# A reordered ramp: powers of lam from the mask's rows, small operations on GpSimd, wide row sums, unread products ahead of a norm

## The chip, the cores and the metric

The kernel runs on one core of a Trainium2 chip. The time is that of one execution in device microseconds, and the number that counts is the median of several runs.

## The reference, cut to what matters

A retention layer (linear attention with a decay lam per head, four sequences of 768 positions, eight heads of 64) is followed by a normalised, gated MLP over all 3072 rows of 512 numbers.

```python
# per head, block b of 64 positions; Dmask[i, j] = lam**(i-j) for i >= j, else 0
intra = ((qb @ kb.T) * Dmask) @ vb
inter = (qb * lam**(pos + 1)) @ kv_state
out[b] = intra + inter
kv_state = lam**64 * kv_state + (kb * lam**(63 - pos)).T @ vb
...
# x: 3072 x 512, the heads' outputs side by side
rms = sqrt(mean(x * x, axis=-1) + 1e-06)
xn = x / rms * rms_g
y = (silu(xn @ w_gate) * (xn @ w_val)) @ w_out          # 512 -> 1536 -> 512
```

## The kernel before, in words

The 3072 rows are six groups m of 512 (four chunks of 128). The 1536 hidden features are twelve blocks f of 128. A unit (m, f) is `Hidden`: `gate` and `val` each multiply a weight block by x in three parts of four passes (part 0: high weight by high x, part 1: low weight by high x, part 2: high weight by low x; f16 halves), `silu` and `mul` join them, `high` and `low` split the product again, and `out` adds it, for each t of four row chunks, to the accumulators acc in PSUM.

The attention of a group is done by `Pair` (m, p), two heads at a time: `scores` (tile pa), `decay_a` (pa times the mask, into a), `decay_k` and `decay_q` (k times lam's power of the last position, q times the powers pw), `state_sums` (pst), `states` (the running state, chunk after chunk), `mix_chunks` (a times v into po), `mix_states` (state times q, added to po), `keep_output` (po into x) and `keep_squares` (po squared, into sq). `scores` of all pairs use one PSUM buffer with the tag ps.

`Norm` makes xn: row sums of the squares (pss), `mean`, `root` (a power on GpSimd, into y), `spread` (y over the partitions by matmuls, pr), and for each block kk of 128 columns `scaled` (xn), `high` (a cast by ScalarE) and `low` (the rest, a subtraction).

`Weights` f turns the raw 64-bit weights into f16 halves: `lift` (ScalarE), `convert` (VectorE, two instructions), `square` and `norm` (a sum of squares, pn), `scale`, `high` (ScalarE), `low` (VectorE), `undo` (two tiny operations that make cg, the factor taken back behind the gate); `lift_o`, `convert_o`, `high_o`, `low_o` do the same for the output weights.

Before the steady loop stands `ramp`: the first two groups' attention, the conversion of the first weights and the units (0, 0) to (0, 5), written out call by call. The order of the calls is the order of each engine's instructions, since the schedule is manual. An engine takes them strictly in that order, and waits at each for its operands. `load_next` issues the next transfer of the list `pending` on SyncE's queue; the tile it loads to is one of four buffers with the tag in, which must be free.

`powers` makes the mask's rows (lam to the power of the distance) and the powers pw by VectorE's scans. `busy(n)` issues n products of the identity with itself into a PSUM tile (unread) that nothing reads.

The ramp ends with the gate of the first unit of group 1; from there on the loop runs the remaining units, and the order there is the same in both kernels.

Of the kernel before, what the change touches and what calls it, by code (L numbers as in the profile page):

```python
# [23 lines left out]
def retention_swiglu_kernel(  # L24
# [117 lines left out]
    def busy(n):  # L142

        ps = ps_out.tile([P, DM], F32, tag="po2", name="unread")
# [10 lines left out]
    def powers(p, part):  # L155
        if part < 2:
            h = 2 * p + part
            nc.vector.tensor_tensor_scan(
                mask[:, h, :], lam_b[:, h : h + 1].broadcast_to([P, P]), ident, 0.0,
                ALU.mult, ALU.add,  # L160
            )
        else:
            nc.vector.tensor_tensor_scan(
                pw[:, p, :], lam_p[:, p : p + 1].broadcast_to([P, P]), zeros, 1.0,
                ALU.mult, ALU.add,
            )
# [23 lines left out]
    def scales_of(pmax):  # L190
        nc.vector.tensor_reduce(gmax, pmax[:, :P], axis=mybir.AxisListType.X, op=ALU.max)
        nc.vector.tensor_single_scalar(ge, gmax.bitcast(I32), 0x7F800000, op=ALU.bitwise_and)
        nc.vector.tensor_scalar_min(ge, ge, float(252 * EXP))
        nc.vector.tensor_scalar(sx.bitcast(I32), ge, -1.0, float(253 * EXP), ALU.mult, ALU.add)
        nc.vector.tensor_scalar(gs, gcol, sx, XS, ALU.mult, ALU.mult)
        nc.vector.tensor_scalar_add(cx.bitcast(I32), ge, float(EXP))
        nc.vector.tensor_scalar_mul(cx, cx, 1.0 / (XS * WS))
# [15 lines left out]

    zeros = wg[:, NF - 1, 1].bitcast(F32)[:, :P]
    nc.scalar.mul(zeros, ones, 0.0)
# [142 lines left out]
    class Weights:  # L358
# [79 lines left out]
        def undo(self):  # L438
            inv = small.tile([P, 2], F32, tag="inv", name=f"inv_{self.f}")
            nc.vector.tensor_scalar_add(inv.bitcast(I32), self.e2, float(64 * EXP))  # L440
            nc.vector.tensor_scalar_mul(cg[:, self.f, :], inv, cx)
# [19 lines left out]
    class Pair:  # L461
# [48 lines left out]
        def states(self):  # L510
            m, p = self.m, self.p
            for c in range(GC):
# [4 lines left out]
                if g % SEQ_CH == 0:  # L517
                    nc.vector.tensor_copy(new, self.pst[:, c, :])
                else:
# [49 lines left out]
        def keep_squares(self):  # L569
# [4 lines left out]
            if m and p == 0:  # L574
# [10 lines left out]

    class Norm:


        def __init__(self, m):
            self.m = m  # L590
            self.x, self.sq = rows.pop(m)
# [6 lines left out]
        def sums(self, i=0):  # L598

            if i == 0:  # L600
                if self.m:
                    pss = ps_att.tile([P, 2, G], F32, tag="ps", name=f"pss_{self.m}")[:, 0]
                else:
                    pss = ps_out.tile([P, DM], F32, tag="po2", name=f"pss_{self.m}")
                self.pss = pss
            sq = self.sq[i]

            n = 1 if self.m else P
            for c in range(GC):
                nc.tensor.matmul(  # L610
                    self.pss[:, c * n : (c + 1) * n], sq[:, c, :], ones[:, :n],
                    start=i == 0 and c == 0, stop=bool(i or self.m), skip_group_check=True,
                )
            self.pss4 = self.pss[:, : GC * n].rearrange("p (c i) -> p c i", c=GC)[:, :, 0]

        def mean(self):
            m = self.m
            self.ms = small.tile([P, GC], F32, tag="ms", name=f"ms_{m}")
            nc.vector.tensor_scalar(self.ms, self.pss4, 1.0 / DM, 1e-6, ALU.mult, ALU.add)
# [197 lines left out]
    def ramp():  # L817
# [7 lines left out]
        powers(0, 0)  # L825
        powers(2, 0)
# [506 lines left out]
```

## Time and profile before

| | us |
|---|---|
| median of 3 runs | 677.46 (677.24 to 678.6) |
| the profiled execution, its time | 678.01 |
| its span, first to last instruction | 676.2 |
| TensorE busy | 666.9 |
| VectorE busy | 324.1 |
| ScalarE busy | 248.4 |
| GpSimd busy | 72.2 |

An execution's time is 1.8 us above its span. A timeline row is a run of like instructions of one engine on one tile: start, duration of the row, engine, line, operation, tiles, shapes, count, and in brackets the idle time ahead of it with what ended it. A matmul's duration holds its way through the array, so rows overlap by up to 0.2 us, and the cost of a row to TensorE is the distance from its start to the next row's start. An f32 matmul appears as two passes.

### The profile page before, as it was taken

Reading aid. Unit: us, or ns where it says so; the run is one execution under the profiler, and the core shown is the slowest. Engines: PE = TensorE matmul, PEld = TensorE weight load, DVE = VectorE, ACT = ScalarE, POOL = GpSimd, SP = SyncE. Lnnn points to the kernel's source line nnn. Section 1 sums busy time; section 2 is a strip of 40 time slices with the busy share of each in tenths; the row PEclk is TensorE's granted clock in tenths of the full one; section 3 lists DMA queues with packets and bytes.
Section 4 is the critical chain, followed back from the end, with each engine's and each line's share of the span. In section 5 each row is a group of like instructions: output and inputs, shape, how many; then the busy total and the mean of one; then the engine's idle time right before and its main releaser. Section 6 shows DMA issues by size and latency. Waiting matters only on the chain.

```text
span 676.2 us, 9894 instructions
## 1 busy us (share of the span) xinstructions
PE 666.9 (99%) x4138; PEld 356.3 (53%) x4138; DVE 324.1 (48%) x579; ACT 248.4 (37%) x439; POOL 72.2 (11%) x71
## 2 busy tenths in 40 slices
PE   7999999999999999999999999999999999999997
PEld 6845665555566444554444555444465444444443
DVE  6797867777546386332812322631331462211112
ACT  3687636776425435322213222221331221211111
POOL 2300000011214303230000111000011000000000
PEclk9999999999999999999999999999999999999999
DMA  8937702541014201122001122100100000100001
GB/s 319 348 128 271 280 25 94 188 156 63 1 63 165 86 0 63 64 94 94 1 0 54 30 105 78 48 0 1 63 1 1 1 0 1 63 0 1 0 1 63
DMA packets 14300, 50.97 MB, mean 75 GB/s; under 512 B 1712, under 2 KB 1968, under 8 KB 12848
## 3 DMA queue, kind: packets, MB, share of 16 engines
q1 hardware_dynamic: 13968, 49.69, 20.4%
q10 hardware_dynamic: 288, 0.66, 0.3%
q8 instruction: 32, 0.52, 0.3%
q14 instruction: 12, 0.10, 0.1%
HBM read 44.05 MB, written 6.29 MB: 74 GB/s over the span
## 4 chain that ended last, share of the span: by engine, by line
PE 96%; DMA 2%; DVE 1%; ACT 1%; issue 0%; DVEq 0%; SPq 0%
PE pg L696 27%; PE pv L696 27%; PE acc L715 9%; PE acc L717 9%; PE acc L716 9%; PE pa L476 4%; PE po L536 3%; PE po L547 3%; PE pst L505 2%; DMA raw_gv<-in_weights_dram 1%; PE unread L146 1%; DMA cs<-in_consts_dram 1%; PE pss L610 0%; DVE xn L674 0%; PE acc L712 0%; PE pr L632 0%
## 5 line engine op out<-in xcount | busy, mean ns | idle before, releaser
L696 PE MATMUL pg<-x,wg 128*128 128x512 f16 x864 | 199.7, 379 | 0.6 <-ACT x L679 0.6
L696 PE MATMUL pv<-x,wv 128*128 128x512 f16 x864 | 199.5, 379 | 0.0
L788 DVE SCALAR_TENSOR_TENSOR sg<-pv,cv,sg 128x512 f32<-128x512 f32 x54 | 40.5, 749 | 241.7 <-PE pv L696 241.7
L696 PEld LDWEIGHTS <-wv 128*128 128x128 f16 x864 | 84.1, 98 | 100.6 <-issue 1.1
L696 PEld LDWEIGHTS <-wg 128*128 128x128 f16 x864 | 82.8, 98 | 102.5 <-issue 4.8
L717 PE MATMUL acc<-wo,hh 128*128 128x512 f16 (+1 forms) x284 | 108.7, 383 | 0.0
L716 PE MATMUL acc<-wo,hh 128*128 128x512 f16 (+1 forms) x284 | 108.7, 383 | 0.0
L781 ACT ACTIVATE sg<-pg,cg 128x512 f32<-128x512 f32 x72 | 49.3, 684 | 160.6 <-PE pg L696 160.5
L798 ACT CAST hh<-sg 128x512 f16<-128x512 f32 (+1 forms) x71 | 43.8, 617 | 162.6 <-DVE sg L788 162.5
L715 PE MATMUL acc<-wo,hh 128*128 128x512 f16 x216 | 82.1, 380 | 0.0
L805 DVE TENSOR_TENSOR hh<-sg,hh 128x512 f16<-128x512 f32 x54 | 38.0, 705 | 27.4 <-ACT hh L798 27.4
L496 POOL TENSOR_TENSOR qkv<-qkv,pw 128x512 f32<-128x512 f32 x21 | 27.0, 1287 | 224.0 <-PE pa L476 220.3
L715 PEld LDWEIGHTS <-hh 128*128 128x128 f16 x216 | 21.1, 98 | 26.6 <-issue 2.8
L717 PEld LDWEIGHTS <-hh 128*128 128x128 f16 x216 | 21.1, 98 | 25.5
L716 PEld LDWEIGHTS <-hh 128*128 128x128 f16 x216 | 21.2, 98 | 23.4
L492 DVE TENSOR_TENSOR a<-pa,mask 128x1024 f32<-128x1024 f32 x24 | 29.3, 1223 | 7.8 <-PE pa L476 7.8
L715 PE MATMUL acc<-wo,hl 128*128 128x512 f32 x68 | 30.4, 446 | 0.0
L476 PE MATMUL pa<-qkv 64*128 64x128 f32 x384 | 28.8, 291 | 0.0
L476 PEld LDWEIGHTS pa<-qkv 64*128 64x128 f32 x384 | 24.1, 193 | 8.3 <-issue 6.6
L567 ACT COPY x<-po 128x512 f32<-128x512 f32 x24 | 13.8, 582 | 31.7 <-PE po L547 31.7
L536 PE MATMUL po<-a,qkv 128*64 128x128 f32 x384 | 25.3, 274 | 0.0
L486 ACT ACTIVATE qkv<-qkv,mask 128x256 f32<-128x256 f32 x48 | 21.7, 503 | 7.5 <-DMA qkv<-in_qkv_dram 7.5
(132 smaller groups left out, 591.3 us busy)
## 6 DMA issues: line engine op xcount, KB each, us to landing
qkv<-in_qkv_dram SPq DMA_DIRECT2D x47, 512.0 KB, 4.7
raw_gv<-in_weights_dram SPq DMA_DIRECT2D x11, 1024.0 KB, 6.1
raw_o<-in_weights_dram SPq DMA_DIRECT2D x12, 512.0 KB, 3.7
out_dram<-o SPq DMA_DIRECT2D x23, 256.0 KB, 2.3
partial<-in_weights_dram SPq DMA_DIRECT2D x2, 512.0 KB, 11.6
qkv<-in_qkv_dram ACTq DMA_DIRECT2D x1, 512.0 KB, 4.2
out_dram<-o SPq DMA_DIRECT2D x1, 128.0 KB, 2.1
out_dram<-o ACTq DMA_DIRECT2D x1, 128.0 KB, 1.9
```

The source lines that it names most:

```text
L476: nc.tensor.matmul(self.pa[:, j, c, :], self.kT[r, c, :], self.qT[r, c, :], start=True, stop=True,)
L492: nc.vector.tensor_mul(self.a, self.pa, decay.broadcast_to([P, 2, GC, P]))
L496: eng.tensor_mul(self.qT, self.qT, pw[:, p : p + 1, :].broadcast_to([P, GC, P]))
L536: nc.tensor.matmul(po[r, c, :], self.v[:, c, r], self.a[:, j, c, :], start=c == 0, stop=False, skip_group_check=True,)
L696: nc.tensor.matmul(ps, w[:, kk, :], x[:, kk, :], start=i == kk == 0, stop=i == 2 and kk == NK - 1,)
L715: nc.tensor.matmul(acc, hl[:, ts_], oh, start=first, stop=False)
L716: nc.tensor.matmul(acc, hh[:, ts_], ol, start=False, stop=False)
L717: nc.tensor.matmul(acc, hh[:, ts_], oh, start=False, stop=last)
L781: nc.scalar.activation(self.sg, self.pg, AF.Silu, scale=cg[:, self.f, 0:1])
L788: nc.vector.scalar_tensor_tensor(out, self.pv, factor, self.sg, ALU.mult, ALU.mult)
L798: nc.scalar.copy(self.hh, self.sg)
L805: nc.vector.tensor_sub(self.hl, self.sg, hh)
```

## The change

Only the ramp changes, with the helpers that it calls.

- Pair 0's two halves change queues: q and k now come by ScalarE's queue, k and v by rows by SyncE's.
- Seven unread products stand ahead of pmax; in all there are 18 and not 20, in six places: 7 at the start, 2 behind the first scores, 2 and 3 between the row sums and the norm's `spread`, 4 between the units h0 and h1.
- The powers pw are no longer scanned. Two matmuls per pair copy the mask's first rows over the partitions (`spread_powers`, tile pp), and ScalarE multiplies them by lam (`powers_of`).
- Five operations of `scales_of`, four of six `undo`, four of six `low_o` and two more of the x `low` go to GpSimd; five of the first state copies go to ScalarE.
- The squares of group 0 are no longer added before the row sums: all four tiles are multiplied by 128 equal columns and summed in PSUM (`row_sums`, 16 matmuls and not 8).
- h1's hidden product is split in two like the others, so that its `out` takes three f32r matmuls for each t and not one f32 matmul.
- The calls stand in another order throughout.

```diff
@@ load_qkv
-            queue = nc.scalar if m == 0 and p == 0 and i else nc.sync
+            queue = nc.scalar if m == p == i == 0 else nc.sync
...
-    def powers(p, part):
-        if part < 2:
-            h = 2 * p + part
-            nc.vector.tensor_tensor_scan(
-                mask[:, h, :], lam_b[:, h : h + 1].broadcast_to([P, P]), ident, 0.0,
-                ALU.mult, ALU.add,
...
+    def spread_powers(p):
+
+        ps = ps_out.tile([P, DM], F32, tag="po3", name=f"pp_{p}")
+        for j, r in enumerate(heads):
+            nc.tensor.matmul(
+                ps[r, :P], ident[:, 0:1].broadcast_to([P, D]), mask[:, 2 * p + j, :], start=True, stop=True
             )
...
+    def powers_of(p, ps):
+        nc.scalar.mul(pw[:, p, :], ps[:, :P], lam_p[:, p : p + 1])
...
+    def scales_of(eng):
+        eng.tensor_scalar_min(ge, ge, float(252 * EXP))
+        eng.tensor_scalar(sx.bitcast(I32), ge, -1.0, float(253 * EXP), ALU.mult, ALU.add)
+        eng.tensor_scalar(gs, gcol, sx, XS, ALU.mult, ALU.mult)
+        eng.tensor_scalar_add(cx.bitcast(I32), ge, float(EXP))
+        eng.tensor_scalar_mul(cx, cx, 1.0 / (XS * WS))
...
+    def row_sums(m, i):
+
+        if i == 0:
+            if m:
+                ps = ps_att.tile([P, 2, G], F32, tag="ps", name=f"pss_{m}")[:, 0]
+            else:
+                ps = ps_out.tile([P, DM], F32, tag="po2", name=f"pss_{m}")
+
+            n = 1 if m else P
+            pss[m] = ps[:, : GC * n].rearrange("p (c i) -> p c i", c=GC)
+        n = pss[m].shape[2]
+        for c in range(GC):
+            nc.tensor.matmul(
+                pss[m][:, c, :], rows[m][1][i][:, c, :], ones[:, :n],
+                start=i == 0 and c == 0, stop=bool(i == NP - 1 or m), skip_group_check=True,
+            )
...
@@ ramp
+        powers(7)
         largest()
+        powers(3)
+        busy(2, 3)
+        powers(0)
+        busy(5)
+        powers(1)
         pm = scales()
...
-        p01.add_squares(nc.gpsimd)
-        p02.add_squares(nc.vector)
...
+        row_sums(0, 2)
+        row_sums(0, 3)
+        busy(2, 3)
...
+        busy(3, 1)
+        w0.norm(slice(1, 2))
...
+        n0.spread()
...
-        busy(3)
-        busy(8)
...
-        h1.mul(True)
+        h1.mul()
```

The order on TensorE, from the first instruction to the second pair's scores, is before (pmax is the product behind the largest scale, pa the scores, pst the state sums):

```order
L187 MATMUL pmax<-ident,gmax 128x128
L146 MATMUL unread<-ident 128x128 x5
L476 MATMUL pa_0_168<-qkv_0_97 128x128 x8
L146 MATMUL unread<-ident 128x128 x4
L505 MATMUL pst_0_187<-qkv_0_97 64x64 x8
L476 MATMUL pa_1_200<-qkv_1_100 128x128 x8
```

and of the changed kernel:

```order
L146 MATMUL unread_147<-ident 128x128 x2
L146 MATMUL unread_151<-ident 128x128 x5
L192 MATMUL pmax<-ident,gmax 128x128
L480 MATMUL pa_0_165<-qkv_0_97 128x128 x8
L146 MATMUL unread_176<-ident 128x128 x2
L165 MATMUL pp_182<-mask,ident 64x128 x2
L509 MATMUL pst_0_186<-qkv_0_97 64x64 x8
L480 MATMUL pa_1_198<-qkv_1_100 128x128 x8
```

The five unread products that stood behind pmax are seven ahead of it, and those behind the first scores are two, with the first spread of powers behind them.

From the row sums of group 0 to its first gate TensorE had before (pss is the row sums, pn a weight norm, pr the spread norm, po the pair's output):

```order
L610 MATMUL pss_372<-ones,sq_0_302 128x128 x4
L610 MATMUL pss_372<-ones,sq_3_364 128x128 x4
L476 MATMUL pa_0_390<-qkv_0_361 128x128 x8
L146 MATMUL unread<-ident 128x128 x11
L412 MATMUL pn_422<-ssq_381,ones 128x2
L632 MATMUL pr_437<-ident,y_435 128x128 x4
L412 MATMUL pn_422<-ssq_426,ones 128x1
L505 MATMUL pst_0_448<-qkv_0_361 64x64 x6
L536 MATMUL po_0_474<-a_0_403,qkv_0_361 64x128 x8
L412 MATMUL pn_493<-ssq_426,ones 128x1
L547 MATMUL po_0_474<-qkv_0_361,state 64x128 x6
L696 LDWEIGHTS wg
```

and of the changed kernel, behind the row sums of the first tile of squares, which stand further ahead:

```order
L612 MATMUL pss_298<-ones,sq_1_290 128x128 x4
L612 MATMUL pss_298<-ones,sq_2_380 128x128 x4
L612 MATMUL pss_298<-ones,sq_3_382 128x128 x4
L146 MATMUL unread_403<-ident 128x128 x2
L416 MATMUL pn_406<-ssq_384,ones 128x1
L146 MATMUL unread_416<-ident 128x128 x3
L416 MATMUL pn_406<-ssq_384,ones 128x1
L645 MATMUL pr_431<-ident,y_424 128x128 x4
L480 MATMUL pa_0_438<-qkv_0_281 128x128 x8
L509 MATMUL pst_0_451<-qkv_0_281 64x64 x6
L416 MATMUL pn_406<-ssq_458,ones 128x1
L709 LDWEIGHTS wg
```

Six unread products fewer stand ahead of pr, the scores of pair (1, 0) went behind it, and the pair's two rows of po went behind the first gate's four passes and the units h0 and h1.

On GpSimd the changed kernel has behind the second q (L500) the five operations of the scales, then the fourth q and the power:

```order
L500 TENSOR_TENSOR qkv_2_103<-qkv_2_103,pw 128x512
L200 TENSOR_SCALAR ge<-ge 128x1
L201 TENSOR_SCALAR sx<-ge 128x1
L202 TENSOR_SCALAR gs<-cs,sx 128x4
L203 TENSOR_SCALAR cx<-ge 128x1
L204 TENSOR_SCALAR cx<-cx 128x1
L500 TENSOR_TENSOR qkv_3_106<-qkv_3_106,pw 128x512
L636 TENSOR_TENSOR y_424<-ms_422,power 128x4
```

All of these but the q and the power were VectorE's before.

## Rows read from the trace of the kernel before

**Rows 1.** The page: TensorE's busy time and share, and the granted clock in 40 slices.
```profile
PE 666.9 (99%) x4138; PEld 356.3 (53%) x4138; DVE 324.1 (48%) x579; ACT 248.4 (37%) x439; POOL 72.2 (11%) x71
...
PEclk9999999999999999999999999999999999999999
```

**Rows 2.** Timeline of TensorE, from its first matmul (start, duration, operation).
```profile
4.61 0.77 PE L187 MATMUL pmax<-ident,gmax 128*128 128x128 f32 x2 [4.61 <-DVE gmax L180]
5.17 2.34 PE L146 MATMUL unread<-ident 128*128 128x128 f32 x10
7.44 2.08 PE L476 MATMUL pa<-qkv 64*128 64x128 f32 x16
9.45 1.23 PE L146 MATMUL unread<-ident 128*128 128x128 f32 x8
```

**Rows 3.** Timeline of GpSimd and VectorE at the start; last, the page's transfer on ScalarE's queue.
```profile
1.12 0.29 POOL masks.py:199 TENSOR_SCALAR_AFFINE_SELECT ident<-ident 128x128 f32<-128x128 f32 x1
...
4.38 1.68 DVE L158 TENSOR_TENSOR_SCAN mask<-cs,ident 128x128 f32<-128x128 f32 x5
...
9.57 1.22 DVE L492 TENSOR_TENSOR a<-pa,mask 128x1024 f32<-128x1024 f32 x1 [1.30 <-PE pa L476]
...
qkv<-in_qkv_dram ACTq DMA_DIRECT2D x1, 512.0 KB, 4.2
```

**Rows 4.** Timeline of TensorE, attention of group 0 to the first gate.
```profile
17.20 0.87 PE L547 MATMUL po<-qkv,state 64*64 64x128 f32 x12
18.00 1.16 PE L476 MATMUL pa<-qkv 64*128 64x128 f32 x16
19.09 0.69 PE L505 MATMUL pst<-qkv 128*64 128x64 f32 x16
19.60 1.05 PE L536 MATMUL po<-a,qkv 128*64 128x128 f32 x16
...
23.21 2.05 PE L610 MATMUL pss<-ones,sq 128*128 128x128 f32 x16
...
26.28 3.05 PE L146 MATMUL unread<-ident 128*128 128x128 f32 x22
...
34.71 1.24 PE L696 MATMUL pg<-x,wg 128*128 128x512 f16 x5 [0.28 <-ACT x L679]
```

**Rows 5.** Timeline of all engines, from the row sums to the first cast.
```profile
25.30 0.16 DVE L619 TENSOR_SCALAR ms<-pss 128x4 f32<-128x4 f32 x1 [0.54 <-PE pss L610]
25.60 1.02 POOL L623 TENSOR_TENSOR y<-ms,power 128x4 f32<-128x4 f32 x1 [3.80 <-DVE ms L619]
...
29.48 1.13 PE L632 MATMUL pr<-ident,y 128*128 128x128 f32 x8
...
30.64 1.41 DVE L674 SCALAR_TENSOR_TENSOR xn<-x,gs,pr 128x512 f32<-128x512 f32 x2 [0.42 <-PE pr L632]
31.43 0.62 ACT L679 CAST x<-xn 128x512 f16<-128x512 f32 x1 [0.31 <-DVE xn L674]
```

**Rows 6.** Timeline of TensorE, output products: h1's f32 form, then two f32r ones.
```profile
65.54 1.10 PE L712 MATMUL acc<-wg,h 128*128 128x512 f32 x2
...
84.44 0.40 PE L715 MATMUL acc<-wo,hl 128*128 128x512 f32 x1
...
85.14 0.39 PE L715 MATMUL acc<-wo,hl 128*128 128x512 f32 x1
```

**Rows 7.** Busy time by stretch: first gate to ramp's end; columns PE, PEld, DVE, ACT, POOL.
```profile
33.15:95.63 62.48, 61.85 (x406) 37.19 (x405) 51.63 (x103) 40.98 (x76) 1.44 (x3) 1.00 0.55 194
```

**Rows 8.** The issue of raw_gv_3 on SyncE's queue; the raw_gv transfers' landing times to 70 us.
```profile
30.02 0.33 SPq L101 DMA_DIRECT2D raw_gv<-in_weights_dram  x1
...
DMA to landing us min/median/max: 4.8/7.1/9.1
```

**Rows 9.** Timeline of GpSimd and VectorE side by side, near 95 us.
```profile
95.33 1.16 POOL L682 TENSOR_TENSOR x<-xn,x 128x512 f16<-128x512 f32 x1 [10.64 <-ACT x L679]
...
95.80 1.23 DVE L682 TENSOR_TENSOR x<-xn,x 128x512 f16<-128x512 f32 x1
```

More of the change, by code (lines that the diff above doesn't have):

```diff
@@ L889, in ramp @@
[L889 to L890 removed]
         n0.mean()
[L892 to L909 removed]
+        n0.root()
@@ new lines, in ramp @@
+        h0.gate(0)
+        load_next()
+        n0.low(2, nc.gpsimd)
+        w0.high(1)
+        p10.mix_chunks()
+        w1.lift_o()
+        w0.lift_o()
+        p10.first_state(nc.scalar)
+        w1.lift(1)
+        w0.low(0)
+        w0.low(1)
+        n0.low(0, nc.vector)
+        w2.lift()
+        h0.val(0)
+        load_next()
+        n0.low(1, nc.vector)
+        w1.high(0)
+        w2.convert(part=0)
+        h0.gate(1)
+        h0.gate(2)
+        h0.silu()
+        w1.convert(1)
@@ L967, in ramp @@
         w2.norm()
-        h1.silu()
-        w0.convert_o()
-        w2.scale()
+        h1.gate(2)
+        h0.mul()
+        w1.high(1)
+        w2.scale()
+        h1.val(0)
+        w1.low(1)
+        p10.decay_q(nc.gpsimd)
+        w2.high(0)
+        w2.undo(nc.vector)
+        w1.undo(nc.gpsimd)
+        h1.silu()
+        h1.val(1)
+        h2.gate(0)
+        w2.low(0)
+        h2.gate(1)
+        load_next()
+        h2.gate(2)
+        h0.high()
+        w3.lift()
+        p10.states(True)
@@ L1010, in ramp @@
         w3.scale()
-        h1.out(2)
-        p11.state_sums()
-        p11.states()
-        w3.high(1)
-        w4.lift()
-        p11.mix_chunks()
-        w3.high(0)
-        w3.lift_o()
-        p12.scores()
-        p11.decay_q(nc.vector)
-        p11.mix_states()
-        load_next()
-        p11.keep_output(nc.scalar)
-        high_o(2)
-        p11.keep_squares()
-        w4.convert(part=0)
-        h3.gate(0)
-        w3.undo()
-        w3.low(0)
-        load_next()
+        h0.out(0)
@@ L1031, in ramp @@
+        p11.states(True)
+        w3.undo(nc.gpsimd)
+        w3.high(0)
+        h2.val(1)
+        load_next()
+        w4.lift()
+        w2.convert_o()
+        w3.low(0)
+        h3.gate(0)
+        h0.out(3)
+        w4.convert(part=0)
+        p11.decay_q(nc.vector)
+        w3.high(1)
+        h1.high()
+        p12.decay_k()
+        high_o(1)
+        h2.val(2)
+        h2.mul()
         h3.gate(1)
+        w4.convert(part=1)
         h3.gate(2)
-        w4.convert(part=1)
+        h3.silu()
@@ new lines, in ramp @@
+        w3.low(1)
+        h0.out(2)
+        w4.scale()
+        w4.undo(nc.vector)
+        load_next()
+        w4.high(0)
+        p11.keep_output(nc.scalar)
+        h0.out(1)
+        h1.out(0)
+        load_next()
+        p11.keep_squares()
+        p12.states(True)
+        w4.low(0)
+        w3.convert_o()
+        load_next()
+        p12.decay_q(nc.vector)
+        w5.lift()
+        h2.high()
+        h4.gate(0)
+        w4.high(1)
+        h4.gate(1)
+        p13.decay_k()
+        w4.lift_o()
@@ L1101, in ramp @@
+        p13.states(True)
+        h3.high()
+        h3.low()
+        w5.undo(nc.gpsimd)
         p13.mix_chunks()
-        p13.states()
+        low_o(3, nc.gpsimd)
         p13.mix_states()
-        load_next()
-        w6.lift()
-        h5.gate(0)
-        h2.out(3)
-        p12.add_squares(nc.vector)
         p13.keep_squares()
         w5.high(1)
+        high_o(4)
+        h5.gate(0)
         w5.low(0)
-        h5.gate(1)
-        h5.gate(2)
-        p13.add_squares(nc.vector)
-        w5.undo()
@@ L1116, in ramp @@
[L1116 to L1133 removed]
+        p13.keep_output(nc.vector)
+        h2.out(1)
+        h2.out(0)
+        h2.out(3)
+        p13.add_squares(nc.vector)
@@ L1134, in ramp @@
+        row_sums(1, 0)
+        load_next()
+        load_next()
+        h2.out(2)
+        h4.high()
+        w6.lift()
+        low_o(4, nc.vector)
+        h5.gate(1)
+        h5.val(0)
+        w5.convert_o()
+        w5.low(1)
+        n1 = Norm(1)
+        n1.mean()
+        n1.root()
+        h3.out(1)
+        h5.gate(2)
+        high_o(5)
+        h4.low()
+        h3.out(3)
         n1.spread()
         n1.scaled(1)
-        low_o(5, nc.vector)
-        h3.out(1)
+        h5.silu()
         h5.val(1)
```

447 lines of the change are left out of this document (185 added, 262 removed).

## The prediction

> **What bounds the kernel now.** I read the page first, then where TensorE waits, then the timeline of the first 100 us. TensorE is busy for 666.9 of 676.2 us, 99% [rows 1]. So time can be won in three ways only: TensorE starts earlier, does less, or does the same faster. From the ramp's end (the gate at 95.63) the two programs give TensorE the same matmuls in the same order, and I take that part over unchanged. What is left is the ramp, and the question is at which time TensorE reaches its end.
>
> TensorE's first matmul, pmax, starts at 4.61 and waits for nothing but the constants and one reduction behind them. The ten passes of the first five unread products take 2.34 us (0.23 each); the same passes take 3.05 us for 22 later (0.14 each). The first scores take 2.08 us, those at 18.00 take 1.16 us [rows 2, 4]. The granted clock is printed as full throughout [rows 1], but these paces are a factor of two apart: I read them as the 1.2 and the 2.4 GHz level; the first scores still run at the lower one, after 2.8 us of work without a pause, and the row of unread products behind them (1.23 us for 8 passes, 0.15 each) is where it rises, near 9.5. From there on no idle time is printed for TensorE up to the first gate. That does not mean that it works for the result: eleven unread products fill 26.28 to 29.16, while the norm of the first group is being made. At the first gate TensorE waits twice for 0.3 us for ScalarE's casts of x, and its first four passes end at about 34.93 (34.71 and one pass of 0.22) [rows 4].
>
> **The change, part by part.** All sums are made against the profiled execution (678.01 us, span 676.2); the median of the runs shown, 677.46, is 0.55 below it, and I apply the same difference to the median. A measurement of this kernel tells about 0.2%, or 1.35 us, from no change.
>
> *The start.* The identity that unread products read is ready at 1.41 (1.12 and 0.29) [rows 3]. Seven of them now stand ahead of pmax: 14 passes at the slow pace, 0.213 each, fill 1.45 to 4.43, where TensorE idled. pmax waits for one mask scan more (0.33): 4.94. q and k of pair 0 now come by ScalarE's queue, whose transfer took 4.2 us from an issue at 0.73 [rows 3], so they are there at 4.9 and the scores begin at about 5.4 instead of 7.44. Whether they run slow (2.0 us, end 7.45) or fast (1.1, end 6.5) hangs on the clock, and no row shows how it goes with this start; I take an end at 7.1, nearer to slow, since before the scores came at the lower level behind 2.8 us of work and here they come behind 3.0 and a pause of 0.5. VectorE's a (1.22 us, [rows 3]) then ends at 8.35. All scores use one PSUM buffer (ps), so the second pair's start at 8.4. Bounds: 7.9 and 9.2.
>
> *From there to the last row sum.* VectorE makes eight scans and not twelve. In place of four, eight small matmuls spread the mask's rows and ScalarE scales them out of PSUM. No row shows these matmuls; they are four passes per pair, between a quarter of the 16-pass po row (0.98) and two of the 0.11 us row-sum rows more, 0.25 to 0.45: I take 0.32, nearer to the po row, whose shape is the same. Row sums go from 8 matmuls (16 passes in 1.98 us) to 16, which buys off two additions of squares. In the new order TensorE has from the second scores on: 3 scores at 1.09, 4 po chunks at 0.98, 3 pst at 0.51, 4 po states at 0.80, 4 row sums at 0.99, 3 spreads at 0.32 = 3.27 + 3.92 + 1.53 + 3.20 + 3.96 + 0.96 = 16.84 us [rows 4]. I followed VectorE, ScalarE and GpSimd beside it with the durations of their rows and found every operand just in time (the closest are the states of pairs 0 and 3, 0.1 to 0.25 us ahead). So the last row sum ends at 8.4 + 16.84, about 25.25, with bounds 24.7 and 26.0. Before, it ended at the same place, 25.19. So doubling the row sums costs what the earlier start won.
>
> *Row sums to the first gate.* Here is the gain. The mean starts 0.1 after the sums, the power 0.3 later and takes 1.02 [rows 5]: about 26.7. Before, TensorE was then still in its unread products, and pr started at 29.48, 2.86 after the power had ended. Now five unread products and two pn stand in between and end by 26.7, so pr starts at 26.75. As in the rows, xn follows 1.16 after pr's start. The order is now 3, 2, 0, 1, so block 0, which the gate reads first, comes two steps of 0.66 later: 29.23. The cast starts 0.79 after its xn and takes 0.62: the first pass at 30.7, the second a cast later at 31.35, the last of four ends at 32.0 [rows 5]. Against 34.93 that is 2.9 us earlier (bounds 2.1 and 3.5). In TensorE's row a gap of about 1.7 us opens between the last pn (29.0) and 30.7.
>
> *What TensorE still owes then.* Ahead of the gate no longer stand: po chunk of pair (1,0), 0.98; its states, 0.80; and four unread products were put between the gates of h0 and h1, 8 passes or 0.95. Against that the f32 products of h1, two passes for each of four t (1.10 us for one t, so 4.4 for four, less some 0.15 each by which the last pass overlaps with the next row: 3.8), became three f32r matmuls for each t (0.70, and up to 0.1 more where they stand alone: 2.8 to 3.1) [rows 6]; so -0.75. Sum: +2.0 us (1.7 to 2.3).
>
> *Moved without a price.* GpSimd gets five tiny operations for the scales, eight for undo, four low_o and two more low. Their like: 1.02 (the power, four columns) and 1.16 for a low; nothing shows a tiny one, so between 0 and 1.02 each. gs is wanted at 27.9; even with 1.02 each the five, behind the second q, end near 20.3 and the fourth q, queued behind them, at 21.5, where the last states want it. VectorE was busy for 51.63 of the 62.48 us from the first gate to the ramp's end [rows 7] and loses some 4 us there (four low_o, four undo and five state copies against one hl and a keep of x). The second half of w1 is now converted some 7 us later, so the buffer of raw_gv_1 comes free at about 37 and raw_gv_3 is issued then and not at 30.02; landing in 4.8 to 9.1 us [rows 8], that is 42 to 46. ScalarE's lift of w3 is queued at about 43 behind the cast of h0; its delay would be passed to the high half of w2 behind it, which TensorE wants near 48.7, 2.4 us after the lift's start at 46.3 at the latest. No cost, but little cover. Later loads are issued no later than before by this order.
>
> A page bears on the moved operations. First the rows: GpSimd's low at 95.33 took 1.16 us while VectorE ran two of its own, each with two SBUF inputs, in 1.23 at 95.80, its usual pace of 0.6 each [rows 9]. The Trainium skill, GPSIMD Engine Reference, 1. Specifications, says that GpSimd shares its SBUF interfaces with VectorE and contends with its instructions of two SBUF inputs. By these rows VectorE loses nothing, and the sum stays; by the rule VectorE's subtractions beside GpSimd's would last as long as those. I go by the rows and make it a rival.
>
> **Sum.** -2.9 + 2.0 = -0.9; small new waits at operands that come just in time, +0.1: -0.8. Span 675.4, this execution 677.2, median 677.46 - 0.8 = 676.7 us.
>
> **Rivals.**
> *A, clearly faster.* The clock rises before or during the first scores and the operand chains leave the four unread products in time in which TensorE would have waited: the second scores start at 7.9 (-0.5), and 0.4 to 0.9 of the unread products costs nothing. -0.8 - 0.5 - 0.4 = -1.7, 675.8; at best 675.1. For it: TensorE is active from 1.45. Against: I found no wait there longer than 0.1.
> *B, slower: the clock falls in the new gap.* Before, TensorE never paused for more than 0.3 us once it ran fast. Now it pauses 0.5 near 8 and 1.7 ahead of the first gate. At the start TensorE lost 2.5 us to the lower level: 4.9 us, from 4.61 to 9.5, with work for half of it. If the clock falls once more in the gap and as much is lost: -0.8 + 2.5 = +1.7, 679.2. It decides as soon as the loss is over 2.15. For it: no row shows a pause as long as this one. Against: nothing but that the short pauses of before left the pace of the gates alone.
> *C, contention.* VectorE's lows and conversions beside six more GpSimd operations last 1.2 and not 0.65: the casts' chain and w0's low are 0.55 late once or twice, +0.55 to +1.1; 677.4, no change. Together with a late raw_gv_3 (every us beyond 46.3 costs one) it reaches 678.5.
> *D, the early start is not used:* the clock rises as late as before, the first scores and pst run slow, the second scores start at 9.2: +0.8, so 677.5, no change.
>
> **How the numbers follow.** Forecast 0.40, A 0.28, B 0.08, C 0.12, D 0.12. The likeliest is 676.7, with 676.1 to 677.3 as its own range. The range for 8 in 10 leaves out B and the far end of A: 675.2 to 678.3. Faster by over 0.2% (below 676.1): A and a fringe of the forecast, 0.32. Slower (above 678.8): B and a little of C, 0.10. Same: 0.58.
>
> **What would show it.** In the new trace: unread products from about 1.45 and a or the second scores at 8.4; the last row sum ending near 25.25; pr near 26.75; the first gate at 30.7 and its fourth pass ending near 32.0; the first gate of the next group at 94.8 instead of 95.63. Wrong would be: row sums that end after 26, since a q or state was late; idle time on TensorE after 32 of over 0.3 us in one place, above all by the lift of w3 or a low; passes of 0.43 us and more in the first gate.

## The result, and the profile after

The changed kernel takes 681.11 us (median of 4 executions, 680.84 to 681.49), the kernel before beside it 677.35: ratio 1.005, 95% interval 1.0038 to 1.0062. Six more executions of it, in a later run, gave 680.28 against 677.28, ratio 1.0055 (1.0043 to 1.0067). It is slower, where the forecast was 676.7. The profiled execution took 680.9, its span 678.8 against 676.2.

The page of the changed kernel: TensorE's busy time, and the granted clock in 40 slices.

```profile
PE 670.5 (99%) x4172; PEld 360.4 (53%) x4172; DVE 318.0 (47%) x557; ACT 250.4 (37%) x447; POOL 82.2 (12%) x89
...
PEclk9989999999999999999999999999999999999999
```

TensorE is busy for 3.6 us more than in [rows 1], and the third slice of the clock is an 8 where all were 9. The timeline of TensorE, start to first gate, then the first gate of the next group:

```profile
1.45 3.35 PE L146 MATMUL unread<-ident 128*128 128x128 f32 x14 [1.45 <-POOL ident masks.py:199]
...
5.16 1.88 PE L480 MATMUL pa<-qkv 64*128 64x128 f32 x16
...
8.57 1.16 PE L480 MATMUL pa<-qkv 64*128 64x128 f32 x16
...
21.84 2.94 PE L612 MATMUL pss<-ones,sq 128*128 128x128 f32 x24
24.63 0.61 PE L146 MATMUL unread<-ident 128*128 128x128 f32 x4
25.39 0.35 PE L416 MATMUL pn<-ssq,ones 128*128 128x1 f32 x2
26.62 0.94 PE L146 MATMUL unread<-ident 128*128 128x128 f32 x6 [0.88 <-ACT x L579]
27.39 0.28 PE L416 MATMUL pn<-ssq,ones 128*128 128x1 f32 x2
27.53 1.14 PE L645 MATMUL pr<-ident,y 128*128 128x128 f32 x8
...
30.19 0.38 PE L416 MATMUL pn<-ssq,ones 128*128 128x1 f32 x2
32.10 0.38 PE L709 MATMUL pg<-x,wg 128*128 128x512 f16 x1 [1.52 <-ACT x L692]
32.76 0.81 PE L709 MATMUL pg<-x,wg 128*128 128x512 f16 x3 [0.28 <-ACT x L692]
33.49 1.54 PE L548 MATMUL po<-a,qkv 128*64 128x128 f32 x16
34.96 1.89 PE L709 MATMUL pv<-x,wv 128*128 128x512 f16 x4
36.64 2.27 PE L709 MATMUL pg<-x,wg 128*128 128x512 f16 x8
38.75 1.05 PE L146 MATMUL unread<-ident 128*128 128x128 f32 x8
...
98.22 1.04 PE L709 MATMUL pg<-x,wg 128*128 128x512 f16 x4
```

Up to the end of the row sums all goes as forecast, even 0.6 better: scores at 5.16 in place of 7.44 [rows 2], second scores at 8.57, row sums at an end near 24.7. Then the three unread products between the two column norms (the sums of squares pn of the weights) wait 0.88 us for ScalarE's copy of x. pr starts at 27.53, the first gate at 32.10 behind a pause of 1.52, and its four passes end at 33.49, where 32.0 stood in the forecast (34.93 before, [rows 4]). And the 16 passes of po behind it cost 1.47 us from start to next start, not the 0.98 of [rows 4]. The same stretch by windows of 1 us (the number behind POOL's is the granted clock):

```profile
33.00:34.00 1.00, 1.00 (x13) 0.58 (x13) 0.96 (x4) 1.00 (x3) 1.00 (x2) 0.99 0.00 0
34.00:35.00 1.00, 1.00 (x13) 0.67 (x10) 1.00 (x2) 1.00 (x3) 0.33 (x1) 0.50 0.00 0
...
36.00:37.00 1.00, 1.00 (x3) 0.30 (x2) 0.99 (x3) 1.00 (x2) 0.00 (x0) 0.50 0.00 0
37.00:38.00 1.00, 1.00 (x5) 0.45 (x4) 0.97 (x3) 0.33 (x1) 0.00 (x0) 0.80 0.00 0
```

After the pause the clock is at its lower level, 1.2 GHz, from 34 to a little over 37 us, although TensorE is busy all the time. Why the pause came late and long is in the timelines of ScalarE and VectorE, with three rows of GpSimd:

```profile
24.94 0.66 ACT L225 ACTIVATE w<-raw_gv 128x512 f32<-128x512 f32 x1 [0.37 <-DMA raw_gv<-in_weights_dram]
25.51 1.06 ACT L579 COPY x<-po 128x512 f32<-128x512 f32 x2
...
27.71 0.16 DVE L423 TENSOR_SCALAR e<-pn 128x1 int32<-128x1 int32 x1 [2.72 <-PE pn L416]
...
27.97 0.42 DVE L234 TENSOR_SCALAR w<-w 128x512 int32<-128x512 int32 x1
28.42 0.69 DVE L237 SCALAR_TENSOR_TENSOR w<-raw_gv,w 128x512 int32<-128x512 int32 x1
...
29.33 2.72 DVE L687 SCALAR_TENSOR_TENSOR xn<-x,gs,pr 128x512 f32<-128x512 f32 x4
30.11 2.59 ACT L692 CAST x<-xn 128x512 f16<-128x512 f32 x4 [0.17 <-DVE xn L687]
...
15.46 0.19 POOL L201 TENSOR_SCALAR sx<-ge 128x1 int32<-128x1 int32 x1
...
29.61 0.30 POOL L445 TENSOR_SCALAR cg<-inv,cx 128x2 f32<-128x2 f32 x1
30.81 2.27 POOL L695 TENSOR_TENSOR x<-xn,x 128x512 f16<-128x512 f32 x2 [0.90 <-ACT x L692]
```

The three products are written as `busy(3, 1)`: they write the PSUM buffer po1. There lies pair (0, 3)'s po until ScalarE has copied it, and that copy is the second of the row at 25.51, behind a lift that itself waited 0.37 us for its weights. Nobody reads what these products write, yet they wait for the engine that still reads what was there. Behind them stand the second column norm, pr, and on VectorE the conversion of w1 (1.11 us), which stands ahead of xn.

### The profile page after: what moved, and what is told of

It reads as the page before. It is cut to its first block, busy times and chain, and to the rows that moved or that the text cites. A ratio compares the mean times of both kernels' runs of the same rounds, so it can differ in the third digit from the quotient of the medians.

```text
span 678.8 us, 9957 instructions
## 1 busy us (share of the span) xinstructions
PE 670.5 (99%) x4172; PEld 360.4 (53%) x4172; DVE 318.0 (47%) x557; ACT 250.4 (37%) x447; POOL 82.2 (12%) x89
## 4 chain that ended last, share of the span: by engine, by line
PE 95%; DMA 3%; DVE 1%; ACT 0%; issue 0%; DVEq 0%; POOL 0%; SPq 0%
PE pg L709 28%; PE pv L709 28%; PE acc L728 10%; PE acc L730 9%; PE acc L729 9%; PE pa L480 3%; PE po L548 3%; PE po L559 3%; DMA partial<-in_weights_dram 2%; PE pst L509 1%; DMA raw_gv<-in_weights_dram 1%; DMA qkv<-in_qkv_dram 1%; DVE xn L687 0%; PE pss L659 0%; PE unread L146 0%; PE pn L416 0%
## 5 line engine op out<-in xcount | busy, mean ns | idle before, releaser
L730 PE MATMUL acc<-wo,hh 128*128 128x512 f16 (+1 forms) x288 | 110.3, 383 | 0.0
L729 PE MATMUL acc<-wo,hh 128*128 128x512 f16 (+1 forms) x288 | 110.2, 383 | 0.0
L500 POOL TENSOR_TENSOR qkv<-qkv,pw 128x512 f32<-128x512 f32 x20 | 25.7, 1285 | 222.3 <-PE pa L480 210.1
L728 PE MATMUL acc<-wo,hl 128*128 128x512 f32 x72 | 32.2, 447 | 0.0
```

The source lines that it names most:

```text
L500: eng.tensor_mul(self.qT, self.qT, pw[:, p : p + 1, :].broadcast_to([P, GC, P]))
L728: nc.tensor.matmul(acc, hl[:, ts_], oh, start=first, stop=False)
L729: nc.tensor.matmul(acc, hh[:, ts_], ol, start=False, stop=False)
L730: nc.tensor.matmul(acc, hh[:, ts_], oh, start=False, stop=last)
```

## The experiments

Theory: the loss lies in the wait for po1 and in the pause ahead of the first gate, in which the clock falls. Rival: the changed order gives TensorE more work than it won. Four kernels ran beside one another (before: 677.39).

**e1_bank**, the three products into another buffer.

```diff
-        busy(3, 1)
+        busy(3, 0)
```

> The three unread products between the two weight norms are written to another PSUM buffer (po0 and not po1), so that they no longer wait for ScalarE's copy of pair 3's output. Theory (pause): that wait (0.9 us on TensorE) makes the first weight's scale, the conversion behind it on VectorE and so xn late; without it the second pn ends near 26.5 and not 27.67, xn starts near 28.3 and not 29.33, the first gate near 31.0 and not 32.10: 1.0 us faster than the changed kernel, 680.1; if the clock also stays up, 1.7 more, 678.4. Rival (work): the loss is TensorE's longer list of products (8 row sums, po and states behind the gate), and the wait only moves: 681.1, no change.

Measured: 679.27 (677.85 to 681.8, 12 executions), 1.0029 (1.002 to 1.0038). The wait is gone, pr at 25.99, gate at 30.55; the pause of 1.52 stays:

```profile
30.55 0.38 PE L709 MATMUL pg<-x,wg 128*128 128x512 f16 x1 [1.52 <-ACT x L692]
```

The profiled execution shows no fall of the clock and the next group's gate at 95.44. Six of the twelve executions have a mean granted clock of 0.996 or 0.997 and took 679.0 to 680.4; of the six at 0.999 or 1.0, five took 677.9 to 679.3 and one 681.8, the slowest of all. The two groups overlap, so the clock does not make the whole spread of 4 us.

**e2_fill**, the pause filled.

```diff
         w1.scale(slice(0, 1))
+        busy(8, 1)
         h0.gate(0)
```

> Eight more unread products (16 passes, about 1.8 us) stand ahead of the first gate, where TensorE paused from 30.3 to 32.1; nothing else changes. Theory (pause): the clock does not fall at 34, the 3.4 us at half pace are gone, 1.7 us faster than the changed kernel: 679.4, although TensorE has more to do. Rival (work): more products, no gain: 681.1 if they fit into the pause, later by what does not.

Measured: 679.44 (678.74 to 679.96, 8 executions), 1.003 (1.002 to 1.004); all eight executions have a mean clock of 0.999 or 1.0. The first gate begins at 32.16, where it began without the products (32.10):

```profile
30.29 2.03 PE L146 MATMUL unread<-ident 128*128 128x128 f32 x16
32.16 1.26 PE L709 MATMUL pg<-x,wg 128*128 128x512 f16 x4
```

So eight products more made it faster: by 1.7 us against the changed kernel's first median (681.11), by 0.8 against its second (680.28). From the first wide row sum to the next group's gate its trace shows 75.13 us, the changed kernel's two traces 76.38 and 76.35, so 1.2 less. What is left, 2.0 us above before, is not the clock.

**e3_bank_fill**, both (six products).

```diff
-        busy(3, 1)
+        busy(3, 0)
...
+        busy(6, 1)
         h0.gate(0)
```

> Both: the three unread products in another buffer, and six unread products ahead of the first gate. Theory (pause): 1.0 + 1.7 = 2.7 us faster than the changed kernel, 678.4, and the same order of time as before the change. Rival (work): 681.1.

Measured: 678.13 (677.4 to 679.32, 11 executions), 1.0011 (1.0003 to 1.002); every mean clock 0.999 or more. The two repairs win back 2.2 to 3.0 of the 3.0 to 3.8 us lost (against 680.28 and 681.11). A new wait shows in TensorE's timeline:

```profile
30.34 0.38 PE L709 MATMUL pg<-x,wg 128*128 128x512 f16 x1
31.00 0.81 PE L709 MATMUL pg<-x,wg 128*128 128x512 f16 x3 [0.28 <-ACT x L692]
31.74 1.09 PE L548 MATMUL po<-a,qkv 128*64 128x128 f32 x16
...
57.76 0.57 PE L509 MATMUL pst<-qkv 128*64 128x64 f32 x12 [0.71 <-ACT sg L794]
...
95.94 2.33 PE L709 MATMUL pg<-x,wg 128*128 128x512 f16 x10
```

With TensorE 1.75 us further at the first gate, pair (1, 2)'s state sums reach the buffer pg before silu has left it.

**e4_no_gap_products**, the changed kernel without the four products between h0 and h1.

```diff
-        busy(4)
         h1.gate(0)
```

> The four unread products between the units h0 and h1 are taken out (8 passes, 1.0 us in the profile of the changed kernel). Both theories: if nothing waits in their place, 1.0 us faster than the changed kernel, 680.1; if the weights of h1 come just in time behind them, TensorE waits instead and nothing is won: 681.1.

Measured: 679.59 (679.4 to 680.63, 5 executions), 1.0037 (1.0025 to 1.0049). In the trace, h1's gate waits 0.84 us for silu in the place of the 1.00 us of products. Inconclusive by itself, since three of the five executions have a mean clock of 0.997 and the profiled one shows no fall.

**e5_before_no_eleven**, a test on the other side: the kernel before without its eleven products (the row of 22 passes, [rows 4]).

```diff
-        busy(3)
-        busy(8)
```

> The kernel before, without the eleven unread products that stand between its row sums and its column norms (the row of 22 that begins at 26.28 us and takes 3.05). Pause theory: they cover the time in which TensorE would wait for the row sums to become xn, and keep its clock up. Without them the spread waits until about 29.5 as now, the first gate begins where it does (33.15, set by the chain over ms, y, pr, xn and the casts), so the profiled gate of the next group stays within 0.4 of 95.63, and in the executions in which the clock falls in the new gap of about 3 us the time rises by 1 to 2 us: 678 to 679.5 in the median. Rival (these products are work like any other, and the kernel is bound by TensorE's work): 2.9 us earlier, or whatever part of it the chain allows, 675 to 677.

Measured: 678.17 (677.29 to 679.67, 11 executions) against 677.24, 1.0016 (1.0008 to 1.0025). All eleven executions have a mean clock of 0.995 to 0.997. TensorE's timeline and two windows:

```profile
27.66 0.38 PE L412 MATMUL pn<-ssq,ones 128*128 128x2 f32 x2 [2.56 <-ACT junk L408]
27.90 1.73 PE L632 MATMUL pr<-ident,y 128*128 128x128 f32 x8
...
33.16 1.90 PE L696 MATMUL pg<-x,wg 128*128 128x512 f16 x8
```

```profile
28.00:29.00 1.00, 1.00 (x8) 1.00 (x8) 0.93 (x3) 1.00 (x4) 0.00 (x0) 0.64 1.03 422
29.00:30.00 1.00, 1.00 (x9) 0.98 (x10) 0.34 (x1) 0.86 (x3) 0.00 (x0) 0.50 1.17 377
```

So the pause theory holds here too: removing work of 2.9 us makes the kernel 0.9 us slower, and pr runs at the lower clock (1.73 us in place of 1.13, [rows 5]) behind a pause of 2.56. The next group's gate stands at 94.93 in this trace, not within 0.4 of 95.63 as expected, but its row sums begin 1.26 earlier than in [rows 4]; from there to that gate it takes 72.98 us against 72.42.

**e6_bank_fill_no4**, **e7_order**, **e8_real_work**: what keeps e3 above before? e6 is e3 without the four products; e7 is e6 with two pieces of order changed; e8 fills the pauses with pair (1, 0)'s own work.

```diff
@@ e7
+        h0.val(1)
         h1.gate(0)
         w1.low(0)
         p11.decay_k()
-        h0.val(1)
...
-        p12.state_sums()
         p11.mix_chunks()
         p11.mix_states()
+        p12.state_sums()
@@ e8, in addition
-        busy(3, 0)
         w0.norm(slice(1, 2))
+        p10.scores()
...
+        p10.decay_a()
         n0.scaled(3)
...
-        busy(6, 1)
+        busy(2, 1)
+        p10.mix_chunks()
         h0.gate(0)
```

> The changed kernel with the bank of the three products between the two norms changed and six products ahead of the first gate (678.13 in the last runs, next group's gate at 95.94), now also without the four products between the two gates (row of 8, 1.00 us). If they are owed work that nothing hides: 677.1, and the gate at 94.9. If they stand where TensorE would wait anyway (without them it waited 0.84 us for ScalarE's silu of the first block, which holds the bank of the second gate): 678.0, and the gate at 95.8.

> The same as the run without the four products, with two pieces of order changed: the second pass of the first value product stands ahead of the second block's gate, so that it is in the place of the wait for silu, and pair (1,2)'s state sums stand behind pair (1,1)'s mix, so that their wait of 0.71 us for the bank that ScalarE's silu frees lies behind 1.85 us of other work. If the part that the prediction's owed work missed is these waits and the four products, they go: 678.13 - 1.0 - 0.7 = 676.4, gate of the next group at 94.2. If TensorE is behind the chain on VectorE and ScalarE there, the waits appear at the next product instead: 677.5 to 678.1.

> The same as the run before it, with the pauses ahead of the first gate filled by work that is owed anyway in place of unread products: pair (1,0)'s scores between the column norm and the spread (in place of three unread products), its decay ahead of xn on VectorE, and its mix (1.0 us) ahead of the first gate in place of four of the six. First gate as before it, 30.3 to 30.8 (VectorE waits 1.7 us there, so the decay of 1.2 us should cost xn little). Owed work falls by 1.0 us: 676.4 - 1.0 = 675.4 and the next group's gate at 93.2 to 93.7 if TensorE's work bounds what follows; the same as the run before it if VectorE's chain does; later by up to 1.2 us if the decay delays xn in full.

Measured: e6 678.65 (1.0017, 1.0008 to 1.0026), e7 677.89 (1.001, 1.0001 to 1.0019), e8 678.34 (1.0014, 1.0005 to 1.0023), before 677.24. From the first wide row sum to the next group's gate the traces show 74.81 us in e3 (21.13 to 95.94), 74.85 in e6 (22.05 to 96.90), 73.82 in e7 (21.13 to 94.95) and 75.09 in e8 (21.13 to 96.22). So the four products cost nothing that a wait for silu (0.84) does not take in their place; e7's order removes both waits and wins 1.0 us in the trace, of which the medians confirm no more than a part. e8 was a miss. The decay of 1.21 us, moved ahead of xn, makes the first gate later (30.76, in e7 30.35). And TensorE, which no longer has po behind the gate's four passes, waits 0.69 us for a low part of x. Ahead of that part VectorE makes the two low halves of w0's weights; beside GpSimd's decay of q they took 1.41 and 1.77 us, in e7 1.54 and 0.74:

```profile
30.88 1.41 DVE L438 SCALAR_TENSOR_TENSOR wg<-w,sc,wg 128x512 f16<-128x512 f32 x1
32.22 1.77 DVE L438 SCALAR_TENSOR_TENSOR wv<-w,sc,wv 128x512 f16<-128x512 f32 x1
...
31.71 1.73 POOL L500 TENSOR_TENSOR qkv<-qkv,pw 128x512 f32<-128x512 f32 x1
```

**e9_after_again**, the changed kernel once more.

> The changed kernel itself, in more executions and beside the two kernels below. The four executions so far took 680.8 to 681.5 us, two with a mean granted clock of 0.997 and two with 1.0, so that the clock's fall (1.7 us in the profiled one) cannot be all of the difference between those and the run with filled pause (679.4, every execution at 0.999 or 1.0). If the pause ahead of the first gate costs by the clock alone: executions at 0.999 or above at about 679.4, those at 0.997 at about 681. If something besides the clock takes the time: both near 681, and a profile without the fall shows where (a late weight transfer ahead of ScalarE's copies, or a longer wait of the three unread products).

Measured: 680.28 (679.68 to 682.41, 6 executions). Five have a mean clock of 0.996 or 0.997 (679.85 to 682.41), one 1.0 (679.68). In the profiled one the products waited 0.41 us, not 0.88, and the clock is 0.50 from 32 to 35. With the first four executions, three at a mean clock of 1.0 took 679.7, 680.8 and 681.3, seven at 0.996 or 0.997 took 679.9 to 682.4. The groups overlap, by their spans too (677.8, 678.4 and 678.9 against 678.1 to 679.6); in one execution of each (681.3 and 682.4) 2.9 us lie outside the span and not 1.8. What takes the time in those without a fall of the mean clock stays open, as none of them was profiled.

**e10_start_only** and **e11_start_small_gpsimd**: the early start alone, in the kernel before; e11 with the small operations on GpSimd as well.

```diff
-            queue = nc.scalar if m == 0 and p == 0 and i else nc.sync
+            queue = nc.scalar if m == p == i == 0 else nc.sync
...
         largest()
+        busy(7)
         pm = scales()
...
         p00.decay_k()
-        busy(5)
...
         p00.scores()
-        busy(4)
...
         p01.decay_a()
         scales_of(pm)
+        busy(4)
@@ e11, five times
-        nc.vector.tensor_scalar...
+        nc.gpsimd.tensor_scalar...
```

> The kernel before with the early start alone: the queues of the first two transfers swapped as in the change, seven unread products ahead of the maximum in place of five behind it, and the four behind the first scores put behind the second. Everything behind that is as before. If the change's loss lies in what it moved behind the first gate, the early start keeps its gain here: first scores at about 5.2 in place of 7.44, decay of the first scores at 8.3 in place of 9.57 (VectorE's scans end at 8.27), so row sums and first gate 1.2 to 2.5 us earlier and 675.0 to 676.2. Rival (the start hides behind VectorE's chain, which has 2.2 us of idle time between 9.57 and 24, or behind the transfers): first gate within 0.4 of 33.15, 677.0 to 677.4.

> The same as the run before it, with the five small operations between 14.08 and 14.93 us on GpSimd in place of VectorE (five of 0.15 to 0.23, 0.9 us in all), as in the change. If VectorE's chain bounds the way to the first gate: 0.5 to 0.9 less than the run before it. If TensorE's work or the transfers do: the same within 0.3. If GpSimd's queue is in the way (its small operations delay a decay of q that a mix waits for): up to 1 us more.

Measured: e10 678.65 (676.26 to 682.0, 12 executions), 1.0024 (1.0009 to 1.004); e11 678.24 (677.0 to 682.95, 11), 1.0035 (1.0018 to 1.0051); before 677.28. Both fall in two groups. In e10 the six executions with a mean clock of 0.999 took 676.3 to 677.8, the six at 0.994 to 0.997 took 679.5 to 682.0 (as an estimate, that clock over a span of 676 us is 2.0 to 4.1 us of full speed lost); in e11 six at 0.998 or more took 677.0 to 678.2, five at 0.995 to 0.997 took 679.6 to 683.0. The profiled execution of e10 is of the first group. Its first gate begins at 32.41, 0.74 earlier than before and so between the two expectations, neither of which had the fall of the clock. Its second scores wait for VectorE's first decay, which comes behind twelve scans and holds the scores' only buffer:

```profile
9.40 1.16 PE L476 MATMUL pa<-qkv 64*128 64x128 f32 x16 [1.65 <-DVE a L492]
```

In e11's trace, also of the first group, the same wait is 1.03 us.

**e12_start_filled** and **e13_start_scans** try the pause and the scans by themselves.

```diff
@@ e12, on e10
         p00.states()
+        busy(6)
         p01.scores()
...
-        busy(4)
         p01.state_sums()
@@ e13, on e11 (ahead of the first scores only the scans of pairs 0 and 1; their order is not shown)
-        powers(2, 0)
...
         p00.states()
+        busy(2)
         p01.scores()
         p01.decay_a()
+        for p in (2, 3):
+            for part in range(3):
+                powers(p, part)
         scales_of(pm)
-        busy(4)
+        busy(2)
```

> The kernel before with the early start, whose pause of 1.65 us ahead of the second scores (they wait for VectorE's first decay, which holds their bank) is filled with six unread products, in place of the four behind the second scores. In the run without the fill the executions fell in two groups: 676.3 to 677.8 at a mean granted clock of 0.999, and 679.5 to 682.0 at 0.994 to 0.997. Pause theory: the second group goes, and with the four products gone from the path the second state sums come 1.1 us earlier, so 676.3 to 676.9 with nearly every execution at 0.999 or above. Rival (the spread comes from elsewhere, as from the transfers): both groups stay, median 678 to 679.

> The kernel before with the early start, the small operations on GpSimd, and the scans of pairs 2 and 3 behind the second decay, so that the first decay follows the first scores (about 7.0 in place of 7.54 or 8.15) and the pause ahead of the second scores is short (two unread products stand there, two behind the second scores). If the scans in front held the early start back: row sums 1.5 to 2 us earlier than in the run with small operations on GpSimd (21.86), first gate at 30 to 30.5, 675.3 to 676.0. If the transfers of the third and fourth pair pace the way (their decays of k begin at 11.85 and 14.5 us): 0.5 us earlier, 676.6 to 677.2.

Measured: e12 676.72 (676.02 to 678.08, 11 executions), 0.9995 (0.9986 to 1.0004); e13 677.35 (677.2 to 678.23, 11), 1.0009 (1.0 to 1.0018); before 677.08. The second group is gone from both: all 22 executions have a mean clock of 0.999 or 1.0. e12 leaves a wait of 0.79 us ahead of the second scores; its trace is of its slowest execution (678.08), with one more wait of 1.16 us at 58.32, for ScalarE's high half of a weight. For e13 the expected gain did not come: its row sums begin at 21.67, e11's at 21.86. Its gate of the next group stands at 94.10, but pair (0, 2)'s states wait 0.65 us for GpSimd's decay of q, queued behind the small operations.

**e14_start_placed**: small operations on VectorE again, and the scans in its idle stretches.

```diff
@@ on e13
         powers(1, 2)
+        powers(2, 0)
+        powers(2, 1)
...
         p00.states()
+        powers(2, 2)
         busy(2)
...
         p01.decay_a()
+        for part in range(3):
+            powers(3, part)
         busy(2)
...
         p02.decay_a()
+        scales_of(pm)
```

> The kernel before with the early start, the small operations on VectorE, pair 2's scans in VectorE's two idle stretches of the run before (1.06 us ahead of the first decay, 0.48 ahead of the second), pair 3's behind the second decay, and the small operations behind the third decay, so that GpSimd's decay of q is not queued behind them (the run before waited 0.65 us for it). If that wait and the scans were what held the early start: next group's gate about 93.4 to 93.8 in place of 94.10, and 675.4 to 676.2. If the way is paced by the transfers, or the ends of the first and the last transfer decide: 676.5 to 677.3, no different from before.

Measured: 675.94 (675.54 to 676.72, 11 executions) against 676.97, 0.9985 (0.9976 to 0.9994); all mean clocks 0.999 or 1.0. This is faster than both kernels. In its timeline TensorE has no wait over 0.3 us behind the identity's:

```profile
8.31 1.16 PE L476 MATMUL pa<-qkv 64*128 64x128 f32 x16
...
20.93 2.05 PE L610 MATMUL pss<-ones,sq 128*128 128x128 f32 x16
...
32.43 1.24 PE L696 MATMUL pg<-x,wg 128*128 128x512 f16 x5 [0.28 <-ACT x L679]
...
93.54 2.77 PE L696 MATMUL pg<-x,wg 128*128 128x512 f16 x12
```

Row sums begin 2.28 us earlier than in [rows 4], the gate 2.28, the next group's gate 2.09 (95.63 before). The medians differ by 1.0 us and not by 2.1, since the profiled execution of before (678.01) is itself 1.0 above the median beside e14. So an early start is worth its time when nothing is given back for it.

## Why the prediction was wrong

- *The start* was right: unread products from 1.45, second scores at 8.57 for 8.4. The row sums ended at 24.7, at the good end of the bounds: the list of TensorE's rows from the second scores on took 16.1 us and not 16.84.
- *Row sums to the first gate* failed, twice. "Five unread products and two pn stand in between and end by 26.7, so pr starts at 26.75" followed their operands and forgot their output, whose buffer is ScalarE's to free: pr at 27.53. And "xn follows 1.16 after pr's start" took the distance from before, where w1's conversion was done ahead of pr; here it took 1.80. xn came 1.42 late and the fourth pass 1.5 late, though the row sums had ended 0.6 early. From their end to the fourth pass it was 8.86 us where the forecast had 6.75; e1, with only the buffer changed, shows 7.82. So the buffer is 1.0 of the 2.1, and VectorE's order (pr to xn still 1.79 in e1) most of the rest.
- *Rival B*, given 0.08, did occur in the profiled execution, and by the mean clock in seven of ten. The gap was forecast (1.7, measured 1.52), the fall of the clock made a rival only because no row showed it. Its price was below the 2.5 taken from the start: by the rows behind the gate 1.47 - 1.03 for po, 1.68 - 0.87 for four passes of pv, 2.11 - 1.73 for eight of pg, 1.6 in all (e3's rows and twice its four passes as the pace without a fall); in e9's trace about as much. By itself it would not have decided: -0.8 + 1.6 is 678.3. And it is not all of the loss, as the three executions without it took 679.7 to 681.3. Without the fall TensorE meets other waits: in e1 0.16 us, in e2 0.7 and in e3 0.9, for a low part of x and for silu. So from the fourth pass to the next group's gate the three took 63.50, 63.96 and 64.20 us, the changed kernel 64.73: behind the gate the fall cost 0.5 to 1.2 net.
- *What TensorE still owes*, +2.0: from the fourth pass to the next group's gate 64.73 us against 60.70, less 1.6 for the clock +2.4; with the waits that come in the clock's place, +2.8 to +3.5 in e1, e2 and e3. Left out were column norms that now stand behind the gate (10 passes and not 8); what they cost was not tested.
- *The sum*: -0.8 + 1.5 + 1.6 + 0.4 = +2.7; the spans of the profiled executions differ by 2.6. The medians differ by 3.8, because the profiled execution of before was itself 0.66 above the later median (its constants let the first reduction begin at 4.31, against 3.2 to 3.9 in the traces of e10 to e14; the prediction allowed 0.55 for this), while that of the changed kernel was 0.2 below its own.
- *Moved without a price* was right for the tiny operations: they took 0.19 to 0.30 on GpSimd, and nobody waited for them in the changed kernel. e13 shows the cover's end: behind the same five, a decay of q came 0.65 late.
- *Rival C* was weighed by a misreading, and its mechanism did occur. [rows 9] show one subtraction of VectorE in 1.23 us, not two: the 21 others of its form in that trace took 0.68 or 0.69. In the changed kernel the first low half of w0's weights, whose two large inputs lie in SBUF, took 1.52 us beside GpSimd's decay of q, the next, mostly behind it, 0.74:

```profile
94.51 0.69 DVE L682 TENSOR_TENSOR x<-xn,x 128x512 f16<-128x512 f32 x1
...
33.05 1.28 POOL L500 TENSOR_TENSOR qkv<-qkv,pw 128x512 f32<-128x512 f32 x1
...
33.35 1.52 DVE L438 SCALAR_TENSOR_TENSOR wg<-w,sc,wg 128x512 f16<-128x512 f32 x1
34.80 0.74 DVE L438 SCALAR_TENSOR_TENSOR wv<-w,sc,wv 128x512 f16<-128x512 f32 x1
```

The first row is from the trace of before, the others from that of the changed kernel. xn, whose input pr lies in PSUM, kept its 0.74 beside GpSimd's lows. So "VectorE loses nothing" was wrong; w0's low came 0.78 late, where C had 0.55. In this trace TensorE does not wait for the low part of x behind it; in e1, e2 and e3 it does, for 0.16 to 0.17. The contention that the Trainium skill, GPSIMD Engine Reference, 1. Specifications, names is thus seen in this case, beside GpSimd's subtraction and its decay of q.
- *Rival D*'s slow first scores did occur (1.88 us), and cost less than it said. A's fast ones are seen in the changed kernel itself: in e9's trace they took 1.16 us, and the second scores began at 8.08.

The cause is shown for the buffer (e1) and for the pause (e2, e5, e12). That the price of the pause is the clock alone is shown only where the clock's fall is in the trace. The 0.7 us by which e3 is still above before is argued from what TensorE owes and not shown; what slows the executions without a fall beyond that stays open.

## What to carry to other kernels

A product that nobody reads still has an output: choose its PSUM buffer like an operand, and ask what is queued ahead on the engine that frees it. Work that only keeps TensorE busy belongs where a pause is, and before it is taken out or moved, the pause it leaves must be priced with the clock's fall, as a share of executions. An early start pays when the engine that feeds it (here VectorE's scans) is rearranged for it, and no work is put behind the gate in exchange; here it was 1.0 us of 677. Before an operation goes to GpSimd, look for the VectorE instructions with two SBUF inputs that will run beside it, and read the count at the end of a row: [rows 9] looked like no loss because one instruction was taken for two.

## What the runs showed of the hardware

- A pause of 1.52 us (e1) or 1.65 us (e10) on TensorE, with the clock at 2.4 GHz ahead of it, was followed by a fall to 1.2 GHz in some executions of the same kernel and not in others (6 of 12 in each, by the mean clock); with 2.56 us it fell in all 11 of e5, with 1.03 in 5 of 11 of e11, with 0.79 in none of 11 of e12. The lengths are those of the profiled execution; those of the others are not on record. In the changed kernel's trace the lower level stood from 34.0 to 37.4, with TensorE busy throughout.
- Behind the same seven unread products the first scores took 1.88 us in one trace of the changed kernel and 1.16 in the other, and 1.16 to 1.98 in those of e10 to e14. The page and the windows of the profile print the clock as full there; the clock record kept with the two traces sets in, at full, at 6.68 and at 4.65 us. So the rise comes at a different time in each execution.
- Some instructions of VectorE with two large SBUF inputs took longer beside an instruction of GpSimd: 1.23 us and not 0.68 (before), 1.52 and not 0.74 (changed kernel), 1.77 and not 0.74 (e8, where GpSimd's own took 1.73 and not 1.28). xn, with one of its inputs in PSUM, did not.
- The last stores of 128 KB landed in 1.9 to 2.1 us in most traces, and in 2.7 to 3.0 in those of e11 and e13; there the span behind the next group's gate is 0.8 to 0.9 us longer (581.4 and 581.5 against 580.6).
